# The second part of a weight: an accumulating transfer in place of a VectorE subtraction

## Chip, cores and metric

One core of one Trainium2 chip runs the whole kernel. The metric is device time in microseconds (us), median of three runs. TensorE is PE in the profile (its weight loads PEld), VectorE is DVE, ScalarE is ACT, GpSimd is POOL, SyncE is SP; SPq and POOLq are the queues on which an engine issues transfers.

## The reference

Causal attention over batch 2, 12 heads, 448 tokens and head size 64, followed by two feed-forward layers on the 896 tokens. Everything is float32 in and out.

```python
def _attn_ref(q, k, v):
    scores = scale * np.matmul(q, k.transpose(0, 1, 3, 2))
    scores = np.where(mask, -1000000000.0, scores)
    scores = scores - np.max(scores, axis=-1, keepdims=True)
    attn = np.exp(scores)
    attn = attn / (np.sum(attn, axis=-1, keepdims=True) + 1e-09)
    return np.matmul(attn, v)
def _moe_ref(x, w_gate, w_val, w_out):      # 896 x 768, d_ff 1536
    gate = 1.0 / (1.0 + np.exp(-(x @ w_gate)))
    return gate * (x @ w_val) @ w_out
def _moe2_ref(x, w_in, w_out):              # 896 x 768, d_ff 2048
    h = x @ w_in
    return (h * np.clip(h + 3.0, 0.0, 6.0) / 6.0) @ w_out
```

## The kernel before

A float32 operand is carried to PE as two parts of type float32r: hi, the value rounded to 12 significant bits, and lo, the value minus hi. A product is three PE products, hi by hi, hi by lo, lo by hi (`TERMS`).

**Weights.** They arrive as 64-bit words and are streamed in 68 units of [128, 768]: `load_unit` (line 88, issued by SP) brings a unit of 768 KB; ACT scales its upper words into a tile `b` (`dec_scale`, L105); DVE shifts (L110), clamps (L114), joins (L118) and sets the sign (L124), after which `b` holds the float32 value; ACT rounds it to `hi` (`dec_hi`, L131); DVE subtracts to get `lo` (`dec_lo`, L136). There are three raw tiles, two tiles `b` and four each of `hi` and `lo`. Each unit is used once.

**Attention.** The heads go in 12 pairs. For a pair PE transposes q and k (`tr`), multiplies them to scores (`s`, L279), DVE takes the maxima (`nm`), ACT the exponentials (`pr`, L307), DVE the reciprocal of the sums (`rc`), POOL scales `pr` by it (`s_nrm`, L322: four query tiles, two heads each, called pr below), PE transposes `pr` to `pt` (L335), ACT and DVE split that into `pth` and `ptl`, and PE multiplies by V (`pav`, L362). POOL also splits V of each pair into `vpad` (L234, L241), called V below; it has three such buffers and waits for PE's `pav` to free one.

The order of all this is a list schedule made when the program is built. Every step has an engine and a cost in nanoseconds; `emit_in_order` repeatedly takes, of the steps that can start first, the one of least rank. The first three weight units are decoded inside the attention stage (steps `Wa` to `Wg`, line 447), and PE's first products with units 0 and 1 (steps `F`) are put between the last pairs' work. A changed cost or engine of a step can move other steps too.

**Feed-forward.** From about 125 us of the trace on, units are used one after another: 24 for gate and value (a pair of units per step, one sigmoid), 12 for the first output, 16 for the second layer's input (one activation per unit), 16 for the last output. While PE works on unit u, ACT and DVE decode unit u + 3 (`decode_a`, then `decode_b`), and SP loads unit u + 6. PE's products there are L168 (`halves`) and, for the last 16 units, L651.

Of the kernel before, what the change touches and what calls it, by code (L numbers as in the profile page):

```python
# [8 lines left out]
F32 = mybir.dt.float32  # L9
F32R = mybir.dt.float32r  # L10
# [5 lines left out]
AX = mybir.AxisListType  # L16
PSUM = bass.MemoryType.PSUM

# A float32 operand is carried to the tensor engine as two float32r parts: hi, rounded to 12
# significant bits, and lo = x - hi, which has at most 12 and so is exact.  A product is  # L20
# hi*hi + hi*lo + lo*hi; lo*lo is below half a unit of the float32 product's last place.
TERMS = ((0, 0), (0, 1), (1, 0))

# float64 weights come as raw 64-bit words.  The upper word read as float32 and scaled by 2**-112
# has the exponent of the float32 value in its low eight exponent bits, three places too far right.
REBIAS = 2.0 ** -112
# The upper word of float32's largest 12-bit value, scaled so: larger magnitudes saturate there.
UPPER_MAX = (1.0 + 0x6FFE00 / 2.0 ** 23) * 2.0 ** (31 - 127)


# [1 line left out]
def kernel(  # L32
# [16 lines left out]
    FF2 = w2_in.shape[1]  # L49
    P = 128  # L50
    CP = 112
    # Query tiles begin where a chunk of D keys does.
    Q0 = [0, *range(S % P or P, S, P)]
    Q1 = [*Q0[1:], S]
    NQ = len(Q0)
# [13 lines left out]
    wtmp = ctx.enter_context(tc.tile_pool(name="wtmp", bufs=2))  # L69
    wsp = ctx.enter_context(tc.tile_pool(name="wsp", bufs=4))  # L70

# [1 line left out]
    units = []  # L73
    for f in range(K1):
        for w in (w_gate, w_val):
# [53 lines left out]
    def dec_hi(u):  # L129
        hi = wsp.tile([P, UN], F32R, tag="hi", name="hi")  # L130
        nc.scalar.copy(hi, part_t[u])  # L131
        split_t[u] = [hi]

    def dec_lo(u):
        lo = wsp.tile([P, UN], F32R, tag="lo", name="lo")
        nc.vector.tensor_sub(lo, part_t.pop(u), split_t[u][0].bitcast(F32))  # L136
        split_t[u].append(lo)

    def decode_a(u):
        if u < NU:  # L140
# [8 lines left out]
    acc_n = [0]  # L149

    def acc():
        """The next of four two-bank accumulators, in turn."""
        pool = psum[acc_n[0] // 2 % 2]
        acc_n[0] += 1
        return pool.tile([P, 2, 512], F32, tag="m", name="m")

    def split(hi, lo, src):
        """src (PSUM or SBUF) into its two parts."""
        nc.scalar.copy(hi, src)
        nc.vector.tensor_sub(lo, src, hi.bitcast(F32))  # L160

    def halves(ps, u, x, k0, first, last, bs=(0, 1), ks=range(6)):
        """ps[f, token] += unit u's [768, 128] block transposed times x, for batches bs."""
        w = split_t[u]
        for i in ks:
            for n, (a, c) in enumerate(TERMS):
                for b in bs:
                    nc.tensor.matmul(  # L168
                        ps[:, b, :S],
                        lhsT=w[a][:, i * P : (i + 1) * P],  # L170
                        rhs=x[c][:, k0 + i, b * S : (b + 1) * S],
                        start=(first and i == 0 and n == 0),
                        stop=(last and i == 5 and n == 2),
                    )
# [4 lines left out]
    xt = [acts.tile([P, KD, NT], F32R, tag=f"xy{x}", name=f"xt{x}") for x in range(2)]  # L179

    with tc.manual_schedule():
        # ================= attention =================
        with ExitStack() as actx:
            def pool(name, bufs, **kw):
                return actx.enter_context(tc.tile_pool(name=name, bufs=bufs, **kw))
# [12 lines left out]
            maskf = const.tile([P, P], F32, name="maskf")  # L198
            maskb = const.tile([P, P], BF16, name="maskb")
            NV = 3  # L200
            # V by chunks of 64 keys, the first head's over the second's, block diagonal.
            vpad = [
                [const.tile([P, NC, P], F32R, name=f"vpad{i}_{x}") for x in range(2)]
                for i in range(NV)
# [64 lines left out]
            def s_pe(p, ts):  # L269
                both = ps_a.tile([P, 2, 512], F32, tag="m", name="s")  # L270
                off = 0
                for t in ts:
                    rows, n = Q1[t] - Q0[t], Q1[t]
                    ps = both[:rows, :, off : off + n]
                    off += n
                    for i, (a, c) in enumerate(TERMS):
                        for j in range(2):
                            r = slice(j * D, (j + 1) * D)
                            nc.tensor.matmul(  # L279
                                ps[:, j],  # L280
                                lhsT=live["q" + "hl"[a], p][r, Q0[t] : n],
                                rhs=live["k" + "hl"[c], p][r, :n],
                                start=(i == 0),
                                stop=False,
                            )
                    for j in range(2):
                        # Half a tile: in the rows of the array that the head's products use.
                        r = slice(j * D, (j + 1) * D) if rows == D else slice(rows)
                        nc.tensor.matmul(  # L289
                            ps[:, j, Q0[t] :], lhsT=identb[r, r], rhs=maskb[r, r],  # L290
                            start=False, stop=True,
                        )
                    live["s", p, t] = ps
# [32 lines left out]
            def c_pe(p, g):  # L326
                ps = ps_pt.tile([P, 512], F32, tag="pt", name="pt")
                for c, off in GROUPS[g]:
                    for t in range(NQ):
                        if Q1[t] > c * D:  # L330
                            # From the middle of a tile: its rows turned by half, and what comes
                            # after the second half is written over or not used.
                            r, rows = max(0, c * D - Q0[t]), Q1[t] - Q0[t]
                            o = off + Q0[t] + r - c * D
                            nc.tensor.transpose(  # L335
                                ps[:, o : o + rows],
                                live["pr", p, t][:, c].rearrange("p j d -> p (j d)"),
                                identf[:rows, r : r + rows],
                            )
                live["pt", p, g] = ps  # L340
# [36 lines left out]
            def x_lo(p):  # L377
                nc.vector.tensor_sub(x_out(p, 1), live.pop(("pav", p)), x_out(p, 0).bitcast(F32))

            # Chunks that share a PSUM bank, with their columns there: the longest left, and the  # L380
            # longest that still fits.
            GROUPS, WIDTH, chunks = [], [], list(range(NC))
            while chunks:
                GROUPS.append([])
# [5 lines left out]
                        chunks.remove(c)  # L390
            NG = len(GROUPS)

            # Query tiles that share a tile of scores, a bank for each head.
            STILES = [(0, 1), (2,), (3,)]

            def product(cols, stationary=P):
                """The weight of a product: its columns, or the load of its stationary operand."""
                return max(cols / 2.4 + 3, stationary / 1.2)

            # Every step of a pair: (key, engine, weight, what it follows, function).  # L400
            steps = []
            for p in range(NP):
                def add(key, eng, ns, after, fn, *args):
# [38 lines left out]
            for i in range(WARM):  # L442
                steps.append(((0, f"Z{i:02}"), "pe", 300, [], z_pe, (0,)))

            # While the last pairs drain: the first weights, and batch 0's part of their products.
            first_acc = []
            for u in range(3):
                w = f"{u}"
                def add(key, eng, ns, after, fn, *args):
                    steps.append(((NP - 3, key + w), eng, ns, after, fn, (u, *args)))  # L450

                def own(*keys):
                    return [(NP - 3, key + w) for key in keys]

                add("W", "sp", 2000, [], load_unit)
                add("Wa", "act", 740, own("W"), dec_scale)
                add("Wb", "dve", 470, own("W"), dec_shift)
                add("Wc", "dve", 470, own("Wa"), dec_clamp)
                add("Wd", "dve", 870, own("Wb", "Wc"), dec_join)
                add("We", "dve", 870, own("Wd"), dec_sign)  # L460
                add("Wf", "act", 740, own("We"), dec_hi)
                add("Wg", "dve", 870, own("Wf"), dec_lo)

            def f_pe(u, i):
                if i == 0:
# [8 lines left out]
                         f_pe, (u, i))  # L474
                    )

            # Buffers: how many, and (step that takes one, step that gives it back) in turn.
            def every(*uses):
                return [((p, a), (p, z)) for p in range(NP) for a, z in uses]

# [20 lines left out]
            HOP = 200  # L501

            def emit_in_order(rank):
                """Emit the steps as a list schedule would start them: of those that can start
                first, the one of least rank."""
                left = {s[0]: s for s in steps}
                eng_of = {s[0]: s[1] for s in steps}
                need = {key: set(s[3]) for key, s in left.items()}
# [30 lines left out]
                p, name = key  # L539
                return p + LATE[name[0]]  # L540

            # How far a kind of step falls back, in pairs.
            LATE = {
                "J": 1.3, "C": 0.07, "R": -0.94, "E": 0.6, "T": -2.37, "H": 1.3, "S": -0.1,
                "X": 1.38, "M": -2.4, "V": 0.28, "N": 1.41, "D": 2.66, "L": 0.0, "W": 0.85,
                "F": 9.0, "Z": 99.0,
            }

            # The tensor engine's clock rises under load: products of zeros keep it busy while the
            # first pairs start.  # L550
            idle = const.tile([P, 512], BF16, name="idle")
            nc.vector.memset(idle, 0.0)
            idle_ps = ps_pt.tile([P, 512], F32, tag="pt", name="pt")
# [12 lines left out]
            for u in range(3):  # L566
                load_unit(u + 3)

        # ================= feed-forward =================
        LA = 3  # L570
        gact = ctx.enter_context(tc.tile_pool(name="gact", bufs=1, reuse_waits="tile"))
        scr = ctx.enter_context(tc.tile_pool(name="scr", bufs=1, reuse_waits="tile"))
# [71 lines left out]
        for c in range(2):  # L644
# [14 lines left out]
            for s in range(NS - 2):  # L659
# [5 lines left out]
                    block(t, s, split_t[u])  # L665
                advance(u)
                u += 1
            # The last two units go by token tile, so that the tiles are done one after another.
            advance(u)
            for t in (0, 2, 4, 6, 1, 3, 5):  # L670
                for i in range(2):
# [41 lines left out]
```

## Time and profile before

| | |
|---|---|
| device time, median of 3 runs | 624.47 us (624.44 to 624.48) |
| span of the profiled execution | 620.4 us |
| time around the span, up to that median | 4.07 us |
| PE, DVE, ACT, POOL busy | 611.8, 413.4, 267.0, 94.3 us |
| granted TensorE clock over the span | 1.000 |
| transfers, mean rate over the span | 105 GB/s |

The profiled execution has no timed value of its own beside its span; the three runs are other executions of the same program. A share of busy time is a mean over stages: POOL's 94.3 us lie in the first 115 us, and PE's idle time lies in the attention stage and in the last few microseconds. The granted clock is a fraction of full speed; it stays at full speed throughout.

### The profile page before, as it was taken

Reading aid. Unit: us, or ns where it says so; the run is one execution under the profiler, and the core shown is the slowest. Engines: PE = TensorE matmul, PEld = TensorE weight load, DVE = VectorE, ACT = ScalarE, POOL = GpSimd, SP = SyncE. Lnnn points to the kernel's source line nnn. Section 1 sums busy time; section 2 is a strip of 40 time slices with the busy share of each in tenths; the row PEclk is TensorE's granted clock in tenths of the full one; section 3 lists DMA queues with packets and bytes.
Section 4 is the critical chain, followed back from the end, with each engine's and each line's share of the span. In section 5 each row is a group of like instructions: output and inputs, shape, how many; then the busy total and the mean of one; then the engine's idle time right before and its main releaser. Section 6 shows DMA issues by size and latency. Waiting matters only on the chain.

```text
span 620.4 us, 8945 instructions
## 1 busy us (share of the span) xinstructions
PE 611.8 (99%) x3498; PEld 560.2 (90%) x3498; DVE 413.4 (67%) x604; ACT 267.0 (43%) x532; POOL 94.3 (15%) x152
## 2 busy tenths in 40 slices
PE   8999999999999999999999999999999999999997
PEld 4788788999999999999999999999999999999997
DVE  6699997556666666666655666788778888617701
ACT  3898998533333333333233222444454443223200
POOL 4889998300000000000000000000000000000000
PEclk9999999999999999999999999999999999999999
DMA  7664350013333333333333333333333345416102
GB/s 167 139 172 124 76 167 3 1 51 102 107 124 125 103 102 107 123 120 109 103 102 101 102 101 102 102 101 110 119 125 108 101 107 169 135 48 196 46 1 89
DMA packets 80489, 65.05 MB, mean 105 GB/s; under 512 B 34624, under 2 KB 76352, under 8 KB 80448
## 3 DMA queue, kind: packets, MB, share of 16 engines
q1 hardware_dynamic: 80448, 64.50, 35.0%
q8 instruction: 27, 0.44, 0.3%
q14 instruction: 14, 0.11, 0.1%
HBM read 61.73 MB, written 2.75 MB: 104 GB/s over the span
## 4 chain that ended last, share of the span: by engine, by line
PE 94%; POOL 2%; DVE 1%; ACT 1%; issue 1%; DMA 0%; SPq 0%; POOLq 0%; DVEq 0%
PE m L168 61%; PE m L651 19%; PE pav L362 5%; PE s L279 3%; PE pt L335 3%; PE s L289 1%; PE tr L247 1%; POOL pr L322 1%; DVE vpad L562 1%; POOL vpad L241 1%; ACT pr L307 0%; DMA q<-in_q_dram 0%; POOL vpad L234 0%; DVE kl L263 0%; DVE ql L263 0%
## 5 line engine op out<-in xcount | busy, mean ns | idle before, releaser
L168 PE MATMUL m<-xt,hi 128*128 128x448 f32 x576 | 142.5, 366 | 0.0
L131 ACT CAST hi<-b 128x768 fp32r<-128x768 f32 x68 | 56.9, 836 | 185.0 <-DVE b L124 162.9
L168 PEld LDWEIGHTS m<-xt,hi 128*128 128x128 f32 x576 | 107.8, 188 | 8.4
L651 PE MATMUL m<-hi,g 128*128 128x384 f32 x448 | 113.8, 334 | 0.0
L168 PE MATMUL m<-yt,hi 128*128 128x448 f32 x384 | 93.4, 365 | 0.0
L136 DVE TENSOR_TENSOR lo<-b,hi 128x768 fp32r<-128x768 f32 x68 | 64.9, 954 | 40.8 <-ACT hi L131 40.8
L168 PE MATMUL m<-xt,lo 128*128 128x448 f32 x288 | 83.8, 365 | 0.0
L651 PEld LDWEIGHTS m<-hi,g 128*128 128x128 f32 x448 | 80.8, 188 | 0.0
L168 PEld LDWEIGHTS m<-yt,hi 128*128 128x128 f32 x384 | 72.1, 188 | 5.7
L651 PE MATMUL m<-lo,g 128*128 128x384 f32 x224 | 74.8, 334 | 0.0
L168 PE MATMUL m<-g,hi 128*128 128x448 f32 x288 | 70.1, 365 | 0.0
L124 DVE SCALAR_TENSOR_TENSOR b<-raw,b 128x768 int32<-128x768 int32 x68 | 65.9, 968 | 2.3
L118 DVE SCALAR_TENSOR_TENSOR b<-b,raw 128x768 int32<-128x768 int32 x68 | 65.4, 961 | 2.3
L105 ACT ACTIVATE b<-raw 128x768 f32<-128x768 f32 x68 | 61.3, 902 | 0.0
L168 PEld LDWEIGHTS m<-xt,lo 128*128 128x128 f32 x288 | 54.1, 188 | 4.3
L168 PEld LDWEIGHTS m<-g,hi 128*128 128x128 f32 x288 | 54.1, 188 | 4.3
L168 PE MATMUL m<-yt,lo 128*128 128x448 f32 x192 | 54.5, 365 | 0.0
L322 POOL TENSOR_SCALAR pr<-pr,rc 64x64 f32<-64x64 f32 (+3 forms) x96 | 52.3, 562 | 8.7 <-DVE rc L316 7.1
L307 ACT ACTIVATE pr<-s,nm 64x64 f32<-64x64 f32 (+3 forms) x96 | 44.4, 469 | 5.9 <-PE s L289 5.2
L605 DVE TENSOR_TENSOR t<-m,t 128x896 f32<-128x896 f32 x12 | 13.1, 1091 | 47.1 <-PE m L168 47.1
L651 PEld LDWEIGHTS m<-lo,g 128*128 128x128 f32 x224 | 42.0, 188 | 0.0
L362 PE MATMUL pav<-pth,vpad 128*128 128x448 f32 (+6 forms) x168 | 41.0, 309 | 0.0
(64 smaller groups left out, 760.1 us busy)
## 6 DMA issues: line engine op xcount, KB each, us to landing
raw<-in_moe_w_out_dram SPq DMA_DIRECT2D x28, 768.0 KB, 4.4
raw<-in_moe_w_in_dram SPq DMA_DIRECT2D x16, 768.0 KB, 4.6
raw<-in_moe_w_gate_dram SPq DMA_DIRECT2D x12, 768.0 KB, 4.5
raw<-in_moe_w_val_dram SPq DMA_DIRECT2D x12, 768.0 KB, 4.3
k<-in_k_dram SPq DMA_DIRECT2D x24, 112.0 KB, 2.7
q<-in_q_dram SPq DMA_DIRECT2D x24, 112.0 KB, 3.0
v<-in_v_dram SPq DMA_DIRECT2D x24, 112.0 KB, 2.9
out_dram<-osb SPq DMA_DIRECT2D x1, 1344.0 KB, 8.5
```

The lines of the kernel that those rows point to most:

```text
L105: nc.scalar.activation(b, words(u)[0].bitcast(F32), AF.Copy, scale=REBIAS)
L118: nc.vector.scalar_tensor_tensor(bi, bi, 3, words(u)[1], op0=ALU.logical_shift_left, op1=ALU.bitwise_or)
L124: nc.vector.scalar_tensor_tensor(bi, words(u)[0], -(2 ** 31), bi, op0=ALU.bitwise_and, op1=ALU.bitwise_or)
L131: nc.scalar.copy(hi, part_t[u])
L136: nc.vector.tensor_sub(lo, part_t.pop(u), split_t[u][0].bitcast(F32))
L168: nc.tensor.matmul(ps[:, b, :S], lhsT=w[a][:, i * P : (i + 1) * P], rhs=x[c][:, k0 + i, b * S : (b + 1) * S], start=(first and i == 0 and ...
L279: nc.tensor.matmul(ps[:, j], lhsT=live["q" + "hl"[a], p][r, Q0[t] : n], rhs=live["k" + "hl"[c], p][r, :n], start=(i == 0), stop=False,)
L307: nc.scalar.activation(pr[:, :, j], ps[:, j].rearrange("p (c d) -> p c d", d=D), AF.Exp, bias=nm[:, j : j + 1], accum_out=sm[:, j : j + 1],)
L322: nc.gpsimd.tensor_scalar(pr[:, :, j], pr[:, :, j], rc[:, j : j + 1], 1.0, op0=ALU.mult, op1=ALU.mult)
L335: nc.tensor.transpose(ps[:, o : o + rows], live["pr", p, t][:, c].rearrange("p j d -> p (j d)"), identf[:rows, r : r + rows],)
L362: nc.tensor.matmul(live["pav", p][:, c * D :], lhsT=vpad[p % NV][a][:, c], rhs=pt[e][:, off : off + S - c * D], start=(c == 0 and m == 0), ...
L651: nc.tensor.matmul(po[t], lhsT=g2[a][:, 2 * s + i, t * P : (t + 1) * P], rhs=w[e][:, i * HC : (i + 1) * HC], start=(s == 0 and i == 0 and ...
```

## The change

`dec_lo` no longer subtracts on DVE. `dec_hi` has ACT write a second tile, the negative of what the first was written from, already rounded to the same type, so that `lo` first holds minus hi; `dec_lo` then has POOL issue a transfer within the chip's SBUF that adds the value `b` to it. The planner's cost of `Wf` on ACT goes from 740 to 1480, and `Wg` moves from DVE (870) to POOL (1500). Comments are taken out elsewhere, which moves line numbers by up to three; the lines of the changed kernel are three higher than those named here from line 137 on.

```diff
     def dec_hi(u):
         hi = wsp.tile([P, UN], F32R, tag="hi", name="hi")
         nc.scalar.copy(hi, part_t[u])
-        split_t[u] = [hi]
+        lo = wsp.tile([P, UN], F32R, tag="lo", name="lo")
+        nc.scalar.mul(lo, part_t[u], -1.0)
+        split_t[u] = [hi, lo]
 
     def dec_lo(u):
-        lo = wsp.tile([P, UN], F32R, tag="lo", name="lo")
-        nc.vector.tensor_sub(lo, part_t.pop(u), split_t[u][0].bitcast(F32))
-        split_t[u].append(lo)
+
+        nc.gpsimd.dma_start(
+            out=split_t[u][1], in_=part_t.pop(u).bitcast(F32R), accum_op=ALU.add
+        )
...
-                add("Wf", "act", 740, own("We"), dec_hi)
-                add("Wg", "dve", 870, own("Wf"), dec_lo)
+                add("Wf", "act", 1480, own("We"), dec_hi)
+                add("Wg", "pool", 1500, own("Wf"), dec_lo)
```

POOL in the middle of attention, before: V of pair 5 (vpad 106 and 107), then pr of pairs 4 and 5, V of pair 6, and so on (x2 is one instruction for each head).

```order
L234 TENSOR_SCALAR vpad_0_106<-v 64x7x64 x2
L241 TENSOR_TENSOR vpad_1_107<-v,vpad_0_106 64x7x64 x2
L322 TENSOR_SCALAR pr<-pr,rc 128x7x64 x2
L322 TENSOR_SCALAR pr<-pr,rc 64x64 x2
L322 TENSOR_SCALAR pr<-pr,rc 128x3x64 x2
L234 TENSOR_SCALAR vpad_0_102<-v 64x7x64 x2
L241 TENSOR_TENSOR vpad_1_103<-v,vpad_0_102 64x7x64 x2
L322 TENSOR_SCALAR pr<-pr,rc 128x5x64 x2
```

The same place now, with the transfer of unit 0:

```order
L237 TENSOR_SCALAR vpad_0_106<-v 64x7x64 x2
L244 TENSOR_TENSOR vpad_1_107<-v,vpad_0_106 64x7x64 x2
L138 DMA lo<-b 128x768
L325 TENSOR_SCALAR pr<-pr,rc 128x7x64 x2
L325 TENSOR_SCALAR pr<-pr,rc 64x64 x2
L325 TENSOR_SCALAR pr<-pr,rc 128x3x64 x2
L325 TENSOR_SCALAR pr<-pr,rc 128x5x64 x2
L237 TENSOR_SCALAR vpad_0_102<-v 64x7x64 x2
```

The transfer stands ahead of the last pr of pair 4, and pr of pair 5 moves ahead of V of pair 6.

POOL two pairs later, before: V of pair 7 (vpad 104 and 105) up to V of pair 8.

```order
L234 TENSOR_SCALAR vpad_0_104<-v 64x7x64 x2
L241 TENSOR_TENSOR vpad_1_105<-v,vpad_0_104 64x7x64 x2
L322 TENSOR_SCALAR pr<-pr,rc 128x7x64 x2
L322 TENSOR_SCALAR pr<-pr,rc 64x64 x2
L322 TENSOR_SCALAR pr<-pr,rc 128x3x64 x2
L234 TENSOR_SCALAR vpad_0_106<-v 64x7x64 x2
```

Now, with the transfers of units 1 and 2:

```order
L237 TENSOR_SCALAR vpad_0_104<-v 64x7x64 x2
L244 TENSOR_TENSOR vpad_1_105<-v,vpad_0_104 64x7x64 x2
L138 DMA lo<-b 128x768
L325 TENSOR_SCALAR pr<-pr,rc 128x7x64 x2
L325 TENSOR_SCALAR pr<-pr,rc 64x64 x2
L325 TENSOR_SCALAR pr<-pr,rc 128x3x64 x2
L138 DMA lo<-b 128x768
L237 TENSOR_SCALAR vpad_0_106<-v 64x7x64 x2
```

Two transfers stand between V of pair 7 and V of pair 8; the work around them keeps its order.

DVE in the same part of the program, before: a sign step (`b<-raw,b`) with a subtraction (`lo`) behind it.

```order
L351 TENSOR_TENSOR ptl<-pt,pth 128x320
L316 RECIPROCAL rc<-sm 128x2
L124 SCALAR_TENSOR_TENSOR b<-raw,b 128x768
L136 TENSOR_TENSOR lo<-b,hi 128x768
L316 RECIPROCAL rc<-sm 128x2
```

Now the sign steps of units 1 and 2 stand together there:

```order
L354 TENSOR_TENSOR ptl<-pt,pth 128x320
L319 RECIPROCAL rc<-sm 128x2
L124 SCALAR_TENSOR_TENSOR b<-raw,b 128x768 x2
L319 RECIPROCAL rc<-sm 128x2
L354 TENSOR_TENSOR ptl<-pt,pth 128x448
```

The subtraction is gone, and unit 2's sign step, two pairs further on before, has moved up.

## Rows read from the trace of the kernel before

**Rows 1.** Page, parts 1 and 4: span, busy time and chain by engine.

```profile
span 620.4 us, 8945 instructions
...
PE 611.8 (99%) x3498; PEld 560.2 (90%) x3498; DVE 413.4 (67%) x604; ACT 267.0 (43%) x532; POOL 94.3 (15%) x152
...
PE 94%; POOL 2%; DVE 1%; ACT 1%; issue 1%; DMA 0%; SPq 0%; POOLq 0%; DVEq 0%
```

**Rows 2.** Stretches: length, busy PE, PEld, DVE, ACT, POOL, clock, DMA share.

```profile
60.00:75.00 15.00, 13.61 (x118) 11.29 (x116) 14.65 (x31) 14.43 (x52) 14.40 (x20) 1.00 0.37 83
75.00:90.00 15.00, 14.95 (x138) 12.47 (x139) 13.59 (x28) 13.25 (x42) 13.28 (x22) 1.00 0.45 134
...
400.00:500.00 100.00, 100.00 (x495) 92.69 (x494) 80.52 (x98) 47.39 (x54) 0.00 (x0) 1.00 0.35 104
```

**Rows 3.** Chain in order of time: start us, us, what.

```profile
72.57 2.43 POOL pr L322 x2
...
125.05 375.22 PE m L168 x1851
```

**Rows 4.** Waits of PE: us in total, times, longest us.

```profile
PE pt L335 <- POOL pr L322: 1.7, 2, 1.4
```

**Rows 5.** Page, part 5: busy us, mean ns of one, idle before.

```profile
L131 ACT CAST hi<-b 128x768 fp32r<-128x768 f32 x68 | 56.9, 836 | 185.0 <-DVE b L124 162.9
...
L136 DVE TENSOR_TENSOR lo<-b,hi 128x768 fp32r<-128x768 f32 x68 | 64.9, 954 | 40.8 <-ACT hi L131 40.8
```

**Rows 6.** Timeline of SP's queue, a weight load: start us, us.

```profile
129.28 0.37 SPq L93 DMA_DIRECT2D raw<-in_moe_w_gate_dram  x1
```

**Rows 7.** Timeline of POOL in attention: start us, us, [idle before].

```profile
64.95 1.80 POOL L322 TENSOR_SCALAR pr<-pr,rc 64x64 f32<-64x64 f32 x1
66.72 0.31 POOL L322 TENSOR_SCALAR pr<-pr,rc 64x64 f32<-64x64 f32 x1
...
71.31 1.15 POOL L241 TENSOR_TENSOR vpad<-v,vpad 64x448 fp32r<-64x448 f32 x1
72.57 0.64 POOL L322 TENSOR_SCALAR pr<-pr,rc 128x448 f32<-128x448 f32 x1
73.19 1.81 POOL L322 TENSOR_SCALAR pr<-pr,rc 128x448 f32<-128x448 f32 x1
...
78.20 0.56 POOL L234 TENSOR_SCALAR vpad<-v 64x448 fp32r<-64x448 f32 x1 [1.14 <-PE pav L362]
...
84.19 1.01 POOL L322 TENSOR_SCALAR pr<-pr,rc 64x64 f32<-64x64 f32 x1
...
91.64 1.47 POOL L322 TENSOR_SCALAR pr<-pr,rc 128x448 f32<-128x448 f32 x1
```

**Rows 8.** Timeline of DVE in attention, decoding steps: start us, us.

```profile
64.42 1.36 DVE L124 SCALAR_TENSOR_TENSOR b<-raw,b 128x768 int32<-128x768 int32 x1
65.70 0.94 DVE L136 TENSOR_TENSOR lo<-b,hi 128x768 fp32r<-128x768 f32 x1
...
73.16 0.94 DVE L136 TENSOR_TENSOR lo<-b,hi 128x768 fp32r<-128x768 f32 x1
74.02 0.55 DVE L114 TENSOR_SCALAR b<-b 128x768 f32<-128x768 f32 x1
...
83.78 1.23 DVE L124 SCALAR_TENSOR_TENSOR b<-raw,b 128x768 int32<-128x768 int32 x1
```

**Rows 9.** Timelines of ACT and of PE in the second layer's input.

```profile
483.42 0.84 ACT L131 CAST hi<-b 128x768 fp32r<-128x768 f32 x1 [1.97 <-DVE b L124]
...
492.81 0.97 PE L168 MATMUL m<-yt,hi 128*128 128x448 f32 x4
```

**Rows 10.** Page, part 6: issues, KB each, median us to landing.

```profile
raw<-in_moe_w_in_dram SPq DMA_DIRECT2D x16, 768.0 KB, 4.6
...
k<-in_k_dram SPq DMA_DIRECT2D x24, 112.0 KB, 2.7
...
out_dram<-osb SPq DMA_DIRECT2D x1, 1344.0 KB, 8.5
```

## The prediction

> **What bounds the kernel now.** I read the page's shares and its chain first. TensorE (PE) is busy 99% of the span and PE work is 94% of the chain that ended last [rows 1]. Then the stretches: from 125 us on the chain is one unbroken run of feed-forward products, 375 us of it from line 168 alone, with the last products behind; between 400 and 500 us PE is busy 100.00 of 100 us, while DVE has 80.5 and ACT 47.4 [rows 2, 3]. So DVE work removed there ends nothing earlier. What is open is the attention stage, before 125 us. There POOL is busy 14.40 of 15 us between 60 and 75 us, ACT 14.43, DVE 14.65, and PE is idle for 1.4 us [rows 2]. The chain runs through POOL's scaling of the probabilities (pr) at 72.57 [rows 3], and PE's largest wait on another engine is for those same pr: 1.7 us in two waits, one of 1.4 us [rows 4]. In that stage POOL and PE are both close to being the bound; after 75 us PE alone is (14.95 of 15).
>
> **The change, part by part.** *Removed:* 68 DVE subtractions at 954 ns, 64.9 us [rows 5]. All but three lie in the feed-forward, beside products that fill PE, and are worth nothing to the end there.
>
> *Added on ACT:* 68 negations of the same shape as the rounding copy, 836 ns each [rows 5], 56.9 us. Sixty-five of them lie where ACT is at most half busy [rows 2]. If that cover were gone they would delay the next activation that frees an accumulator, which the 8.5 us of slack worked out below covers. Three lie in attention: the negations of units 1 and 2, with the rounding of unit 2 brought forward and its scaling, of nearly the same size, done earlier, put two instructions net, 2 x 0.84 = 1.7 us, more on ACT between 60 and 75 us, against 0.57 us of idle time there, so at worst 1.1 us late. The same pr wait for POOL next, which is later still (below), so the two delays overlap and I count POOL's.
>
> *Added on POOL:* 68 issues of an accumulating transfer. No transfer is issued from POOL before, so the time that one takes there is unknown. Low end: 0.37 us, SP's issue of a weight load [rows 6]. High end: 1.81 us, the longest POOL instruction in the stage, one that was held up [rows 7]. I take 1.15 us, POOL's longest instruction when nothing holds it up [rows 7], since descriptors for 128 partitions are real work for it. Sixty-five come when POOL has nothing else (0.00 busy between 400 and 500 us [rows 2]). Three stand in POOL's full stretch: after V of pair 5 (54 us in the trace), after V of pair 7 (72.5 us), and three groups of pr later, before V of pair 8.
>
> *Taken off POOL:* a DVE instruction that reads two SBUF tiles holds POOL up. A 64x64 pr takes 0.31 us alone and 1.80 us at 64.95, beside the sign step (64.42 to 65.78) and the subtraction (65.70 to 66.64); a 128x448 pr takes 0.64 us alone and 1.81 us at 73.19, beside the subtraction that runs 73.16 to 74.10 [rows 7, 8]. Without the subtractions POOL gets about 0.94 us back at each of these two places, and 0.83 us at 91.64 (1.47 against 0.64).
>
> *Moved:* the planner now knows other costs and puts unit 2's sign step next to unit 1's, before V of pair 8; before, it came at 83.78 and cost POOL 1.01 - 0.31 = 0.70 us [rows 7, 8]. That delay now falls before 78 us.
>
> *The sum on POOL up to V of pair 8:* 3 x 1.15 - 2 x 0.94 + 0.70 = +2.27 us. In the trace POOL waits 1.14 us for PE at that point (78.20 [rows 7]); so much is absorbed, and 1.13 us reach PE through the pr that its transposes wait for. After that POOL gains (the stall at 91.64 is gone, and the one at 84.19), but PE has no idle time left in which to make up, so the delay stays. With 0.37 us per issue the sum is -0.07 us and nothing reaches PE; with 1.81 us it is +4.25, so +3.1 us. The span grows from 620.4 to 621.5 us; 4.07 us lie around it up to the median of 624.47, which I keep. Forecast: **625.6 us**.
>
> A rule that speaks against the change: the Trainium skill's page "SBUF — State Buffer" (Who interferes with whom) says that descriptor generation on GpSimd is starved while VectorE is in a two-port mode, which tensor_scalar operations can enter. Here that would be the shift and the clamp; no transfer from POOL has run, so no row shows it. If each of the three issues met one of them, at the 0.55 us of a clamp [rows 8], the sum would be 1.65 us more, 627.2; it is inside the range and I give it no more.
>
> *The wait added in the feed-forward.* PE's third product of a unit now waits for a transfer, and so does the scaling two units on. Tightest is the stage with one activation per unit. There the rounding of a unit starts at 483.42 and takes 0.84, the negation ends at 485.1, and the unit is begun by PE at 492.81; its first product with the second part comes four products (0.81 us) later, at 493.6 [rows 9]. So a transfer has 8.5 us from the negation to landing. Its time from issue to landing is unknown too: 2.7 us (a 112 KB load) and 8.5 us (the 1344 KB store) are the ends, 4.6 us for a 768 KB load is the nearest, since an accumulating transfer reads twice 384 KB [rows 10]. 1.15 + 4.6 = 5.8 us is under 8.5, with 2.7 us to spare: no cost.
>
> The Trainium skill's page "DMA: Bandwidth & Descriptors" (Anatomy of one DMA — SWDGE (gpsimd) path) gives 2.0 us and bytes over 436 GB/s for such a transfer: by estimate 2.9 us for 384 KB, which would also leave the feed-forward at no cost. No row here shows an accumulating transfer, which also reads its target.
>
> **The rivals.** *Relief outweighs issue.* If an issue is near SP's 0.37 us, POOL comes out level or ahead before 78 us, and the 1.7 us that PE waits for pr [rows 4] go, since one of these waits stands right behind the 1.80 us pr. 622.8 us. For it: the stalls are in the rows. Against it: the first issue (54 us) stands 11 us ahead of the first relief (65.7), and POOL builds descriptors in software. It decides below 0.4 us an issue.
>
> *Hidden.* The planner put other PE work (score and value products) into the places where POOL is late, so the 1.13 us never reach PE: 624.5 us. For it: PE's order was redone around the three issues. Against it: POOL and ACT are both over 95% busy from 60 to 75 us, so later pr make later work of every kind.
>
> *Transfers too slow for the feed-forward.* If issue and landing take 1.81 + 8.5 = 10.3 us, they pass 8.5 us by 1.8 us. A unit three ahead depends on the one just ended, so each unit loses a third, 0.6 us, over the 16 units of the tight stage about 9.6 us: 634 us, and more if the other stages join or the 16 DMA engines, 0.35 busy between 400 and 500 us [rows 2], fill up. It decides at 8.5 us from negation to landing, and it is the one that costs most. Against it: twice the time of the nearest row.
>
> **How the numbers follow.** Three runs of before lie within 0.04 us; 0.2% is 1.25 us, what I take a measurement to tell from no change. Forecast case 0.60: its own range is 624.5 to 627.6, and 625.7 cuts it in half, 0.30 within and 0.30 slower. Hidden 0.18, within. Relief 0.10: 0.08 faster, 0.02 within. Slow transfers 0.12, slower. Together 0.08 faster, 0.50 within, 0.42 slower. The range 623.0 to 630.0 holds the forecast case and its bounds, the hidden case and most of the relief case; left out are the slow transfers and the end of the relief.
>
> **What would show it.** In the profile after: about 57 us more on ACT and 65 us less on DVE; three issues on POOL between 50 and 80 us, each near 1.2 us; no POOL instruction at twice its time beside a subtraction; PE's waits for pr up from 1.7 to about 2.8 us; the run of line 168 from the end of attention on takes 375 us as now. It is wrong if an issue is far from 1.15 us, if PE shows waits for a transfer in the feed-forward, or if the first feed-forward run starts before 125 us.

## The result and the profile after

The changed kernel takes 628.51 us (median of 5 runs, 625.88 to 628.77), the kernel before beside it 624.44 us (5 runs, 622.17 to 624.48): ratio 1.0074, 95% interval 1.0051 to 1.0098. It is slower, by 4.6 us at that ratio. Both kernels' times come in steps that go with the mean granted clock of the execution: the kernel before takes 622.2 us at 1.000 and 624.5 us at 0.994, so the profiled span of 620.4 us, at 1.000, belongs to 622.2 us, and 1.8 us lie around it, not the 4.07 us that the prediction took.

The profiled span grows from 620.4 to 626.9 us. The chain of waits of the kernel after, in order of time (start us, us, what; the line that was L168 is now L171, L651 is L654):

```profile
55.05 4.98 DMA lo<-b
...
60.06 0.02 ACT b L105
...
62.66 0.64 DVE ptl L354
...
63.34 1.33 PE pt L338 x5
...
130.84 375.82 PE m L171 x1854
506.67 116.52 PE m L654 x672
```

Against [rows 3] the feed-forward's run is as long as before: its 0.6 us more go with three more products in the same unbroken run (1854 against 1851). It begins 5.79 us later (130.84 against 125.05). The loss lies in the attention stage, and the chain there runs through a transfer. These are the rows of the page after for the new operations (as in [rows 5, 10]):

```profile
L138 POOL DMA_DIRECT2D lo<-b x68 | 66.1, 972 | 414.5 <-ACT lo L133 398.7
L133 ACT ACTIVATE lo<-b 128x768 fp32r<-128x768 f32 x68 | 57.2, 841 | 0.0
lo<-b POOLq DMA_DIRECT2D x68, 384.0 KB, 4.4
```

An issue holds POOL 0.97 us, a negation holds ACT 0.84 us, and a transfer lands 4.4 us after the start of its issue: landings are counted from there, so that the issue is a part of the 4.4 us. Now the place, first ACT (start us, us, instruction, in brackets the idle time before it and what ended it):

```profile
60.06 0.89 ACT L105 ACTIVATE b<-raw 128x768 f32<-128x768 f32 x1 [3.25 <-DMA lo<-b]
60.85 0.52 ACT L310 ACTIVATE pr<-s,nm 128x320 f32<-128x320 f32 x1
```

The scaling of unit 2 takes a tile `b`, of which there are two. It gets the one that unit 0's transfer is reading. That transfer is issued at 55.05 and lands 4.98 us later, at 60.03. ACT stands still for 3.25 us, and behind the scaling stand the exponentials of the next query tile and the copy of `pt` that frees PE's transposes. POOL and PE in the same stretch:

```profile
55.05 0.99 POOL L138 DMA_DIRECT2D lo<-b  x1
56.14 2.93 POOL L325 TENSOR_SCALAR pr<-pr,rc 128x448 f32<-128x448 f32 x6
62.71 1.04 POOL L325 TENSOR_SCALAR pr<-pr,rc 128x320 f32<-128x320 f32 x2 [3.64 <-DVE rc L319]
...
78.83 0.87 POOL L138 DMA_DIRECT2D lo<-b  x1
...
82.60 0.86 POOL L138 DMA_DIRECT2D lo<-b  x1 [0.17 <-issue]
```

```profile
60.35 0.28 PE L365 MATMUL pav<-pth,vpad 128*128 128x64 f32 x1
63.34 1.33 PE L338 MATMUL pt<-identf,pr 128*128 128x128 f32 x5 [2.71 <-DVE ptl L354]
...
67.47 0.57 PE L365 MATMUL pav<-ptl,vpad 128*128 128x448 f32 x1
...
69.97 0.42 PE L365 MATMUL pav<-pth,vpad 128*128 128x384 f32 x1
```

POOL, which the prediction took for the bound, is idle for 3.64 us there, waiting for work that stands behind ACT. PE is idle for 2.71 us, and when it goes on its products are slow: a product of 448 columns takes 0.57 us at 67.47 and 0.36 us at 53.99. The stretches tell why (columns as in [rows 2]; the granted clock stands ahead of the DMA share):

```profile
60.00:62.00 2.00, 0.62 (x6) 0.51 (x5) 0.98 (x2) 1.91 (x5) 0.00 (x0) 1.00 0.79 172
62.00:64.00 2.00, 0.67 (x3) 0.67 (x4) 1.96 (x4) 1.98 (x5) 1.29 (x3) 0.68 0.15 34
64.00:66.00 2.00, 2.00 (x18) 1.50 (x16) 1.94 (x4) 1.30 (x4) 1.83 (x3) 0.50 0.04 8
66.00:68.00 2.00, 2.00 (x11) 1.78 (x10) 1.43 (x5) 1.42 (x6) 1.70 (x3) 0.50 0.00 0
68.00:70.00 2.00, 2.00 (x14) 1.33 (x12) 0.51 (x1) 1.54 (x9) 0.82 (x2) 0.61 0.60 137
70.00:72.00 2.00, 2.00 (x18) 2.00 (x16) 1.81 (x5) 1.43 (x6) 0.82 (x2) 1.00 0.43 97
```

After the idle time TensorE is granted 0.50, the lower of its two levels (1.2 of 2.4 GHz), until about 69.5 us, although it is busy without a break from 63.34 us on.

### The profile page after: what moved, and what is told of

The parts are those of the page before. It is cut to its first block, busy times and chain, and to the rows that moved or that the text cites. A ratio compares the mean times of both kernels' runs of the same rounds, so it can differ in the third digit from the quotient of the medians.

```text
span 626.9 us, 9192 instructions
## 1 busy us (share of the span) xinstructions
PE 615.6 (98%) x3498; PEld 563.3 (90%) x3498; DVE 353.3 (56%) x536; ACT 316.9 (51%) x600; POOL 156.4 (25%) x220
## 4 chain that ended last, share of the span: by engine, by line
PE 90%; ACT 3%; DVE 3%; issue 1%; POOL 1%; DMA 1%; POOLq 0%; DVEq 0%; ACTq 0%
PE m L171 61%; PE m L654 19%; PE pav L365 4%; PE pt L338 3%; PE s L282 3%; ACT pr L310 1%; PE s L292 1%; PE tr L250 1%; DVE vpad L565 1%; DMA lo<-b 1%; ACT pth L348 1%; DVE nm L303 1%; DVE kl L266 0%; DVE ptl L354 0%; POOL vpad L244 0%
## 5 line engine op out<-in xcount | busy, mean ns | idle before, releaser
L138 POOL DMA_DIRECT2D lo<-b x68 | 66.1, 972 | 414.5 <-ACT lo L133 398.7
L171 PE MATMUL m<-xt,hi 128*128 128x448 f32 x576 | 142.5, 366 | 0.0
L171 PEld LDWEIGHTS m<-xt,hi 128*128 128x128 f32 x576 | 107.8, 188 | 8.4
L654 PE MATMUL m<-hi,g 128*128 128x384 f32 x448 | 113.9, 334 | 0.0
L171 PE MATMUL m<-yt,hi 128*128 128x448 f32 x384 | 93.4, 365 | 0.0
L171 PE MATMUL m<-xt,lo 128*128 128x448 f32 x288 | 83.8, 365 | 0.0
L654 PEld LDWEIGHTS m<-hi,g 128*128 128x128 f32 x448 | 80.8, 188 | 0.0
L171 PEld LDWEIGHTS m<-yt,hi 128*128 128x128 f32 x384 | 72.1, 188 | 5.7
L654 PE MATMUL m<-lo,g 128*128 128x384 f32 x224 | 74.8, 334 | 0.0
L171 PE MATMUL m<-g,hi 128*128 128x448 f32 x288 | 70.1, 365 | 0.0
L114 DVE TENSOR_SCALAR b<-b 128x768 f32<-128x768 f32 x68 | 38.2, 562 | 53.0 <-ACT b L105 53.0
L171 PEld LDWEIGHTS m<-xt,lo 128*128 128x128 f32 x288 | 54.1, 188 | 4.3
L171 PEld LDWEIGHTS m<-g,hi 128*128 128x128 f32 x288 | 54.1, 188 | 4.3
L133 ACT ACTIVATE lo<-b 128x768 fp32r<-128x768 f32 x68 | 57.2, 841 | 0.0
L171 PE MATMUL m<-yt,lo 128*128 128x448 f32 x192 | 54.5, 365 | 0.0
L325 POOL TENSOR_SCALAR pr<-pr,rc 64x64 f32<-64x64 f32 (+3 forms) x96 | 48.2, 517 | 18.2 <-DVE rc L319 16.3
```

The costliest lines, as they stand in the source:

```text
L114: nc.vector.tensor_scalar(b, b, UPPER_MAX, -UPPER_MAX, op0=ALU.min, op1=ALU.max)
L133: nc.scalar.mul(lo, part_t[u], -1.0)
L138: nc.gpsimd.dma_start(out=split_t[u][1], in_=part_t.pop(u).bitcast(F32R), accum_op=ALU.add)
L171: nc.tensor.matmul(ps[:, b, :S], lhsT=w[a][:, i * P : (i + 1) * P], rhs=x[c][:, k0 + i, b * S : (b + 1) * S], start=(first and i == 0 and ...
L325: nc.gpsimd.tensor_scalar(pr[:, :, j], pr[:, :, j], rc[:, j : j + 1], 1.0, op0=ALU.mult, op1=ALU.mult)
L654: nc.tensor.matmul(po[t], lhsT=g2[a][:, 2 * s + i, t * P : (t + 1) * P], rhs=w[e][:, i * HC : (i + 1) * HC], start=(s == 0 and i == 0 and ...
```

## The experiments

The theories: A, the scaling of unit 2 waits for unit 0's landing, and PE's idle time brings the clock down; B, the prediction's own, POOL's issues delay its sums; C, the new order of the plan, or ACT's extra negations, cost by themselves; D, the transfers cost in the feed-forward.

### A third tile for unit 2

```diff
...
-        b = wtmp.tile([P, UN], F32, tag="b", name="b")
+        b = (third[0] if u == 2 else wtmp).tile([P, UN], F32, tag="b", name="b")
...
```

(`third[0]` is the pool of the attention stage's constants.)

> The changed kernel with a third tile b for unit 2, so that ACT's scaling of unit 2 no longer shares a tile with unit 0's transfer; every engine's instructions stand in the same order. Theory A (that scaling waits 3.25 us for unit 0's transfer to land, PE then idles 2.71 us and its clock falls to 0.50 for some 6 us): the wait of 3.25 us is gone, the clock stays near 1.00 in 60 to 75 us, the attention ends near 125 to 126 us in place of 130.84, and the time is 622.5 to 625 us. Theory B (POOL's three issues and its delayed sums decide, the step of the prediction): nothing of that depends on the tile, POOL still ends late, 627.5 to 628.8 us. Theory C (the new order of the plan and ACT's negations decide, not the wait): 627 to 628.8 us. Theory D (the transfers of the feed-forward cost): 627.5 to 628.8 us.

Measured: 623.43 us (622.70 to 623.51, 11 runs), ratio to the kernel before 1.0005 (0.9996 to 1.0015). Every instruction stands where it stood. ACT, then PE, then the chain:

```profile
56.77 0.90 ACT L105 ACTIVATE b<-raw 128x768 f32<-128x768 f32 x1
```

```profile
60.40 0.28 PE L365 MATMUL pav<-pth,vpad 128*128 128x64 f32 x1
60.51 0.76 PE L338 MATMUL pt<-identf,pr 128*128 128x128 f32 x5
...
64.44 0.42 PE L365 MATMUL pav<-pth,vpad 128*128 128x384 f32 x1
```

```profile
125.32 375.82 PE m L171 x1854
```

The wait is gone, and with it 125.32 against 130.84: 5.52 us. PE's rows split them. The transposes start at 60.51 in place of 63.34: 2.83 us of waiting. From these transposes to the same value product is 64.44 - 60.51 = 3.93 us here and 69.97 - 63.34 = 6.63 us in the kernel after, with the same products and no idle time in either: 2.70 us of low clock. 2.83 + 2.70 = 5.53. (Both of these executions began with a clock of 0.89 over the first 15 us, so the comparison is even.) Theory A holds. B, C and D fall as they were put, each at 627 us or more: the order is that of the changed kernel, with its negations and its issues, and it loses next to nothing.

The 2.70 us need not be lost in every execution. The fastest of the changed kernel's five, 625.88 us at a mean clock of 0.997, is 2.6 to 2.9 us below the three at 0.991, which is the size of this term; that execution has no trace. The control, with the same third tile in the kernel before:

> Control: the kernel before with the same third tile b for unit 2 and the same order. All theories expect the time of the kernel before, 624.4 us within 0.2%. If it is over 1 us faster, the third tile pays by itself and the first experiment must be read against it.

Measured: 622.25 us (622.20 to 624.69, 12 runs), ratio 1.0001 (0.9987 to 1.0014). The tile is worth nothing where no transfer reads it.

### Either part alone

The third kernel keeps VectorE's subtraction and the plan of before for units 0 to 2; the fourth has the transfer for these alone.

```diff
...
-        nc.gpsimd.dma_start(
-            out=split_t[u][1], in_=part_t.pop(u).bitcast(F32R), accum_op=ALU.add
-        )
+        lo = split_t[u][1]
+        if u >= 3:
+            nc.gpsimd.dma_start(out=lo, in_=part_t.pop(u).bitcast(F32R), accum_op=ALU.add)
+        else:
+            nc.vector.tensor_sub(lo, part_t.pop(u), split_t[u][0].bitcast(F32))
...
```

(The fourth kernel has `u < 3` there, and the planner's costs of the changed kernel.)

> Units 0 to 2 subtract on VectorE as in the kernel before (same plan in the attention), units 3 and on go by the negation and the transfer. Theories A, B and C (all the cost is in the attention): the time of the kernel before, 624.4 us within 0.2%, the attention ends at 125.0 us and the feed-forward's chain keeps 375.2 us. Theory D (the transfers of the feed-forward cost): 627.5 to 628.8 us.

Measured: 624.55 us, 622.26 to 624.63 over 12 runs, ratio 1.0016 (1.0003 to 1.0028). Its fastest runs take 622.3 us, as those of the kernel before do, and in the profiled execution the run of feed-forward products takes 375.22 us, without a wait of PE for a transfer. That execution took 624.54 us, and its attention ends at 127.35 us. Its trace shows why: the kernel before has one gap of PE in mid-attention, for pr [rows 4]; here the same gap stands before the same transposes, but what follows it differs. The gap before, then the gap here and the two stretches behind it:

```profile
75.05 0.33 PE L335 MATMUL pt<-identf,pr 128*128 128x128 f32 x1 [1.43 <-POOL pr L322]
```

```profile
75.83 0.33 PE L341 MATMUL pt<-identf,pr 128*128 128x128 f32 x1 [1.44 <-POOL pr L328]
```

```profile
76.00:78.00 2.00, 2.00 (x11) 1.32 (x11) 0.64 (x2) 1.08 (x2) 1.85 (x4) 0.51 0.05 10
78.00:80.00 2.00, 2.00 (x13) 2.00 (x12) 2.00 (x4) 0.59 (x1) 0.00 (x0) 0.64 0.03 8
```

Before, the clock stays at 1.00 from 75 to 90 us [rows 2]. So a gap of equal length left the clock alone in one execution and was followed by its fall in another. Why 8 of this kernel's 12 executions are at 0.994 or 0.995, and 4 of the 29 of the kernel before beside it, stays open. 65 transfers in the feed-forward cost nothing.

> The opposite: units 0 to 2 go by the negation and the transfer, units 3 and on subtract on VectorE. Theories A, B and C: as the changed kernel, 627.5 to 628.8 us, with the attention's end near 130.8 us. Theory D: the time of the kernel before, 624.4 us within 0.2%.

Measured: 627.75 us (626.81 to 628.65, 6 runs), ratio 1.0076 (1.0060 to 1.0093), with the same wait of ACT, and the attention ends at 129.97 us:

```profile
59.33 0.89 ACT L105 ACTIVATE b<-raw 128x768 f32<-128x768 f32 x1 [3.24 <-DMA lo<-b]
```

The three transfers in attention carry the whole loss.

### The gap filled

```diff
...
+                if (p, g) == (4, 2):
+                    for i in range(14):
+                        nc.tensor.matmul(
+                            live["spare", 5, 2][:, i % 2, 320:], lhsT=idle[:, :P],
+                            rhs=idle[:, :192], start=True, stop=True,
+                        )
...
```

(`live["spare", 5, 2]` is the score tile.)

> The changed kernel with 14 products of zeros (128 x 192) on TensorE ahead of the transposes that wait 2.71 us, written to columns of a score tile that nobody reads; they can begin when ScalarE has done with that tile, some 1.4 us into the gap, and take some 1.4 us. If TensorE's idle time is what brings the clock down (2.70 us lost in the stretch from these transposes to the product that follows at 69.97), the clock stays near 1.00 there, the stretch takes 3.93 us as in the kernel with a third tile, and the time is 625 to 626.3 us (2.7 us less). If the clock falls for another reason, or 1.4 us of idle time are enough for it, 627.5 to 629 us.

Measured: 625.32 us (625.21 to 626.06, 11 runs), ratio 1.0033 (1.0021 to 1.0044). PE, and two of its stretches:

```profile
61.99 1.32 PE L333 MATMUL s<-idle 128*128 128x192 bf16 x14 [1.33 <-ACT pr L311]
63.31 0.76 PE L345 MATMUL pt<-identf,pr 128*128 128x128 f32 x5
...
67.25 0.42 PE L372 MATMUL pav<-pth,vpad 128*128 128x384 f32 x1
```

```profile
64.00:66.00 2.00, 2.00 (x24) 1.71 (x24) 2.00 (x5) 1.86 (x6) 1.84 (x3) 1.00 0.03 8
66.00:68.00 2.00, 2.00 (x18) 1.64 (x17) 2.00 (x6) 1.92 (x9) 1.82 (x3) 1.00 0.51 118
```

The transposes start as late as in the kernel after, 63.31, but the clock stays at 1.00 and the stretch takes 3.94 us. Work that nobody uses, in the second half of the gap, gives back the 2.7 us, and the mean clock is 0.996 or more in all 11 executions, where it is 0.994 or less in four of the five of the changed kernel. So the low clock is a consequence of PE's idle time, and in the profiled execution it is half the loss by itself.

### Telling the planner of the landing

If the plan's ignorance of the landing caused the wait, the plan can be told. First with two tiles:

```diff
                     if eng == "sp":
                         done[key] += 1800
+                    if key[1][:2] == "Wg":
+                        done[key] += 4000
```

> The changed kernel, two tiles b as it has, but the planner counts 4000 for the landing of a transfer behind POOL's 1500, so that it puts ACT's scaling of unit 2 later in ACT's order (17 rows further on, behind unit 1's negation). Theory A (the scaling waited for the landing): no ACT wait for a transfer over 0.5 us and no fall of the clock near 64 us; with a plan that is otherwise no worse than the one with a third tile the time is 622.5 to 624.5 us. Theory B (POOL's issues) and theory C (ACT's negations or the order as such) keep 626 us or more, since the three issues and negations stay.

Measured: 629.02 us (628.27 to 629.51, 6 runs), ratio 1.0086 (1.0069 to 1.0102): theory A's number is wrong here. No engine waits for an accumulating transfer any more, but the whole order is another, and another gap has opened in it, whose releaser the profile doesn't name (issue). PE, DVE ahead of it, and a stretch of PE:

```profile
73.87 0.98 PE L250 MATMUL tr<-identf,k 112*128 112x112 f32 x4 [3.29 <-issue]
```

```profile
69.79 1.78 DVE L124 SCALAR_TENSOR_TENSOR b<-raw,b 128x768 int32<-128x768 int32 x1
71.50 1.74 DVE L303 TENSOR_REDUCE nm<-s 128x2 f32<-128x896 f32 x3
73.16 0.60 DVE L266 SCALAR_TENSOR_TENSOR ql<-tr,qh 128x448 fp32r<-128x448 f32 x1
```

```profile
74.00:76.00 2.00, 2.00 (x11) 1.67 (x11) 1.50 (x4) 1.73 (x8) 2.00 (x5) 0.50 0.52 118
```

The rows suggest what it waits for. The program has one tile `tr`, which PE's transposes of k write at 73.87; DVE's `ql` reads it for q until 73.76, behind a sign step of 1.78 us and three maxima. No run moved that sign step, so this is argued, not shown.

Then with a third tile that the planner knows of, the landing, and 1000 in place of 1500 for POOL's step:

> A candidate: a third tile b for unit 2 that the planner knows of, POOL's step at 1000 in place of 1500 and 4000 for the landing, so that nothing in the plan waits for a transfer and less is counted for POOL. Theory A expects no ACT wait for a transfer and 622.0 to 624.0 us; since TensorE's products set the feed-forward and the attention before ended at 125.05 us with few waits, a gain over the kernel before of more than 0.5 us is not expected by any theory. Theories B and C: 626 us or more.

Measured: 627.07 us (625.78 to 629.50, 6 runs), ratio 1.0059 (1.0038 to 1.0081). Again no wait for an accumulating transfer, and again a gap of PE. The `xt` that ends it starts at 65.12 us on DVE, behind a sign step of 1.23 us at 62.57 and three maxima, and the clock is at 0.50 after it:

```profile
65.87 0.44 PE L365 MATMUL pav<-pth,vpad 128*128 128x448 f32 x1 [1.91 <-DVE xt L381]
```

```profile
68.00:70.00 2.00, 2.00 (x10) 1.70 (x9) 0.45 (x3) 0.96 (x4) 2.00 (x5) 0.50 0.74 168
```

The fastest of its six runs, 625.78 us at a mean clock of 1.000, loses 3.5 us without the low clock.

Three plans with other costs, three different gaps, losses of 3.7 to 5.4 us by the ratios. So theory C is right in one half: the new costs change the order, and each of these orders opened a gap. The order alone does not decide it, since the third tile kept the changed kernel's order and lost nothing; there the gap is the wait for the landing, in the other two it stands behind DVE's decoding.

### The order of before

That leaves the other half of C, the work itself. Here the planner is left at the costs of the subtraction, so that all steps stand in the order of the kernel before:

```diff
...
-                add("Wf", "act", 1480, own("We"), dec_hi)
-                add("Wg", "pool", 1500, own("Wf"), dec_lo)
+                add("Wf", "act", 740, own("We"), dec_hi)
+                add("Wg", "dve", 870, own("Wf"), dec_lo)
...
```

> The changed kernel, two tiles b, with the planner left at the costs of the subtraction (740 on ScalarE, 870 on VectorE), so that the steps stand in the order of the kernel before: the negations stand behind the roundings, the three transfers on POOL where VectorE's subtractions were planned, and ScalarE's scaling of unit 2 stands 11 rows or more behind the transfer of unit 0. Theory A (order and landing, not the work itself): the scaling finds its tile free or waits under 1 us, TensorE has no idle time over 2 us near 60 to 75 us, the clock stays at 1.00, and the time is 622.2 to 624.6 us, as the kernel before. Theory B (POOL's three issues and its delayed sums, the prediction's step): POOL late by about 1.1 us at the sum, 623.4 us in an undisturbed run, as the prediction added. Theory C (ACT's three negations of 0.85 us cost by themselves): 625 us or more.

Measured: 622.11 us (622.03 to 622.86, 12 runs); the kernel before beside it 622.97 us (622.19 to 624.81, 17 runs); ratio 0.9981 (0.9969 to 0.9994). It beats the changed kernel, and the one before by a hair: 622.1 us against 622.2 where the mean clock is 1.000. B's and C's numbers fall. The rest of the ratio lies in the clock: no run of the 12 has a mean under 0.997, where 7 of the other's 17 do. PE's gap of 1.43 us for pr is not in this order (no gap between 20 and 125 us is over 0.43 us), nor in that of the third tile, where none of 11 runs is under 0.997 either; that the gap makes the difference fits these counts and the trace of the third kernel above, and no run shows it alone. POOL, ACT and the chain:

```profile
66.37 0.98 POOL L138 DMA_DIRECT2D lo<-b  x1
...
72.95 1.83 POOL L325 TENSOR_SCALAR pr<-pr,rc 128x448 f32<-128x448 f32 x4
74.72 0.83 POOL L138 DMA_DIRECT2D lo<-b  x1
75.45 1.63 POOL L325 TENSOR_SCALAR pr<-pr,rc 128x192 f32<-128x192 f32 x2
77.42 1.21 POOL L237 TENSOR_SCALAR vpad<-v 64x448 fp32r<-64x448 f32 x2 [0.34 <-PE pav L365]
```

```profile
73.81 0.89 ACT L105 ACTIVATE b<-raw 128x768 f32<-128x768 f32 x1
```

```profile
124.88 375.22 PE m L171 x1851
```

The scaling of unit 2 stands at 73.81 us, 6.46 us after the end of the first issue; nothing waits. POOL is ready for V of pair 8 at 77.42 - 0.34 = 77.08 us; before it was ready at 78.20 - 1.14 = 77.06 [rows 7]. So two issues, 0.98 + 0.83 = 1.81 us, cost POOL nothing, near the 2 x 0.94 us that the prediction read off the stalls beside the subtractions: four pr take 1.83 us together at 72.95, where one took 1.81 us. In this order the change is free; with the new planner costs it was not.

### The slack of the feed-forward

Units 0 to 2 as before; in the others POOL adds zeros first, and the second transfer waits for the first to land.

```diff
...
+            nc.gpsimd.dma_start(
+                out=lo.rearrange("p (a b) -> p a b", a=2),
+                in_=zero[:, None, :].to_broadcast([P, 2, UN // 2]), accum_op=ALU.add,
+            )
             nc.gpsimd.dma_start(out=lo, in_=part_t.pop(u).bitcast(F32R), accum_op=ALU.add)
...
```

> Units 0 to 2 on VectorE as before; for units 3 and on POOL issues two accumulating transfers one behind the other's landing, the first of which adds zeros (384 KB written, the zeros read twice from a tile of half the width). From the negation's end to the second landing that is 2 x (1.0 + 4.4) = 10.8 us against the 8.5 us that the prediction read as slack. If that slack is right, TensorE shows waits for a transfer of about 2.3 us in the feed-forward, or some 0.8 us a unit where three units are in flight, and the time is between 626 and 675 us. If the slack is larger than 10.8 us (the units' order gives more room than one unit shows), no wait shows and the time is 622.2 to 624.6 us.

Measured: 729.51 us (726.52 to 734.18, 4 runs), ratio 1.1682 (1.1649 to 1.1714). Waits of PE (us in total, times, longest), and the page's landings:

```profile
PE m L180 <- DMA lo<-b: 59.6, 29, 4.0
PE m L663 <- DMA lo<-b: 23.5, 6, 5.7
```

```profile
lo<-zero POOLq DMA_DIRECT2D x65, 384.0 KB, 6.1
lo<-b POOLq DMA_DIRECT2D x65, 384.0 KB, 4.8
```

Both transfers were slower than one alone. From the end of the negation to the second landing it takes 12.1 us (median of the 65 units: 0.3 to the first issue, 6.1, 0.5 to the second, 4.8; a landing is counted from the start of its issue, so the 10.8 us expected had counted each issue twice). That is 3.6 us over the 8.5 us of slack, or 1.2 us a unit with three units in flight, and PE's waits for these transfers are 59.6 + 23.5 = 83.1 us, 1.28 us a unit. The loss, some 105 us, is larger than the 50 us that I allowed. Most of the rest goes with the clock, which I had left out: a mean of 0.968 over the span of 732.4 us stands for some 23 us, by estimate (0.032 x 732.4). So at 12.1 us the wait is there, and at the 4.7 us of the changed kernel it is not; where between them it begins no run shows, and 8.5 us stays a reading from the rows.

## Why the prediction was wrong where it was

The direction of the forecast came out, and the time lies inside its range, but that is luck: the forecast's own case ended at 627.6 us even with issues of 1.81 us, and what was lost is not what it had counted. The time was 2.9 us too low; 1.1 us of loss was forecast and 4.6 us measured at the ratio. By its steps:

- *Feed-forward hidden*: right. The run of products takes 375.82 us, no wait of PE for a transfer shows in it, and 4.7 us from the end of a negation to the landing (median of the 68) stands against 8.5. The 4.6 us taken from the 768 KB load was near, 4.4; to add 1.15 to it was a misreading, since a landing is counted from the start of its issue.
- *POOL's issue*: 1.15 us was taken, 0.97 us measured (0.86 to 0.99 for the three in attention).
- *POOL's relief*: right in size, shown in the order of before, where it cancels the issues. In that order the rival that the relief outweighs the issue came half true, at a higher price of an issue than it asked for, since only two issues stand ahead of V of pair 8: POOL is level there (77.08 against 77.06) and PE's wait for pr is gone, but the kernel gains 0.1 us, not 1.7.
- *The sum on POOL, +1.13 us to PE*: did not happen. In the kernel after two of the three issues stand at 78.83 and 82.60 us, and POOL had idle time.
- *The step that failed* is the one on the wait: "PE's third product of a unit now waits for a transfer, and so does the scaling two units on." It was priced for the feed-forward alone, at the tightest place there. In attention the same sentence holds for exactly one scaling, that of unit 2, and the prediction even says that it is "done earlier", but counted only its 0.84 us on ACT ("at worst 1.1 us late"), not what it now had to wait for. What ran in its place, in the profiled execution: 2.83 us of waiting, and 2.70 us of low clock, a term that the prediction had nowhere.
- *The signs asked for*: ACT up by 49.9 us, not 57 (316.9 against 267.0), since the 68 negations take 57.2 us but overlap with their neighbours in the sum, as `hi` at 489.81 us (0.84 us) and the negation at 490.56 do; DVE down by 60.1 us, not 65 (353.3 against 413.4); waits for pr did not grow, the wait of 2.7 us is for `ptl` in place of [rows 4]; the line-171 run is as long as it was.

What stays open: why each of the three re-costed plans opens its gap just there. No run changed a single place of the order.

## What to carry to other kernels

When an instruction becomes a transfer, ask of every buffer that it reads who takes that buffer next, and where that taker stands in its engine's order: the landing time is a wait there even when the consumer of the result has slack. In a kernel whose order comes from a cost table, first try the new operation in the old order; a corrected cost moves everything, and the moved order can cost more than the operation. An idle gap of TensorE can cost twice its length, as it did here (2.83 and 2.70 us): read the granted clock behind it, and in more than one execution where you can.

## What the runs showed of the hardware

- In the traces, idle time of TensorE of 2.71, 3.29 and 1.91 us in the middle of a busy stage was followed by nearly 7 us at a granted clock of 0.50, most of them with TensorE busy. Of two gaps of equal length, 1.43 us in the kernel before was followed by 1.00 [rows 2] and 1.44 us in the third kernel by some 3.5 us at 0.50; 1.33 us in the filled gap was followed by 1.00. So the length of a gap alone does not tell what the clock does, and each of these is one execution. The Trainium skill's page "TensorE: Matmul & The Clock Gate" (What's actually happening) says that the lower level is the default and that activity lifts it. The filled gap agrees, since 1.32 us of products of zeros kept 1.00.
- An issue on POOL takes longer beside VectorE's clamp. In the feed-forward of the kernel after, the 39 issues with VectorE idle take 0.84 to 0.87 us, as at 313.43 us; the 25 with a whole clamp of 0.56 us beside them take 1.16 to 1.26 us, as at 308.41 us. That is the sign that the Trainium skill's page "SBUF — State Buffer" (Who interferes with whom) gives; the size, 0.3 us, is under the 0.55 us that the prediction estimated from it.
- An accumulating transfer of 384 KB within SBUF lands 4.4 us after the start of its issue, 3.5 us after the end of it (medians of 68), where the estimate by the page "DMA: Bandwidth & Descriptors" of the Trainium skill (Anatomy of one DMA — SWDGE (gpsimd) path) was 2.9 us; two of them chained, beside the same weight loads, take 6.1 and 4.8 us.
